# Reordered start rows, a seventh product one step later and copies 32 steps later in a Fourier and token-mixer kernel

## The chip, the cores and the metric

The kernel runs on one core of a Trainium2 chip. The metric is the device time of one execution in microseconds (us). The core has a matrix engine (TensorE, PE in the profile), a vector engine (VectorE, DVE), an activation engine (ScalarE, ACT), GpSimd (POOL) and SyncE (SP), which here only issues DMA transfers. TensorE's weight loads are shown apart as PEld. Each engine works through its own instructions in the order in which the program gives them, and semaphores hold an instruction back until its inputs are there. All transfers share 16 DMA engines.

## The reference

```
xn = layernorm(x)                                    # x: 2048 x 640, over the 640 columns
a = xn @ dft_hid_re.T ;  b = xn @ dft_hid_im.T
fourier = dft_seq_re @ a - dft_seq_im @ b            # 2048 x 640
h = layernorm(xn)
u = gelu(h.T @ w1 + b1)                              # 640 x 1728
mixer = (u @ w2 + b2).T                              # 2048 x 640
out = x + fourier + mixer
```

All arrays are float32.

## The kernel before

Every matrix product is made in three passes (high part times high part, high times low, low times high). ScalarE rounds a 128 x 512 operand to its high part (`high`, line 148), VectorE subtracts to get the low part (`low`, line 151), and TensorE multiplies. Products are grouped by a scheme with seven block products in place of eight; the operands of some are sums or differences of raw blocks, made in place by VectorE (`sub`, line 154). So each raw slice is loaded into `pieces`, perhaps replaced by a difference, then cut into high and low parts.

The work is a list of steps; one step multiplies one cut slice (nine matmuls for products 1, 2, 3 and 5 of a column stage, six for 4, 6 and 7). `turn_of(i)` writes out the work around step i in program order: DMA loads put down for that step, reads of finished PSUM banks, sums, the high part of step i + 2, extras (among them the differences), jobs from a queue, the low part of step i + 2, and last the matmuls of step i. What is late is thus decided by hand-written tables: `JOBS_AT` says in which step of a stage how many queued jobs run, and the numbers in `columns` say when slices are loaded, differences are made and banks are read.

The stages are: a first column block (60 matmuls of 512 columns), written out word by word in the string `START`; eight column stages of the Fourier half (`columns`, g = 0 to 7, 28 steps each, the fourth only 21, beginning at step 5); then hidden-dimension, up and down products. In `columns`, the loads of a stage's slices B11, B21, B12 and B22 are put down from six steps before the stage to four steps into it, into buffers that the stage before frees. The results of a column stage go to DRAM through GpSimd (`store_y`), many of them as accumulating transfers.

In `START`, x k loads row block k of x, b i the i-th first piece and W a slice of the first stage; M and A take a row block's mean and variance on VectorE, R its root on ScalarE, V the factors on GpSimd (four small steps), N normalises the row block, H writes its high part and L its low part; T and B cut piece i into high and low; P multiplies; E and G read finished banks through ScalarE, Y reads them through VectorE; J is a first job of the later sums.

Later row blocks 8 to 15 are loaded in pairs by `later_load` at steps 28, 31, 33 and 35, and their statistics are jobs. The out rows are first filled with x by 16 DRAM-to-DRAM copies of 320 KB on SyncE's queue (line 1174); everything else is accumulated into them later. All SyncE transfers stand in one queue, and the queue holds at an instruction that waits: for a buffer to be freed, or for the transfer eight places before it to land, since eight completion semaphores are used in turn.

Of the kernel before, what the change touches and what calls it, by code (L numbers as in the profile page):

```python
# [11 lines left out]
AF = mybir.ActivationFunctionType  # L12
# [15 lines left out]
H2 = D // 2  # L28
# [15 lines left out]


START = """
    x0 b0 b1 x4 b2 b3 x1 x2 W1-1-0 x3 W1-1-1 x5 W1-1-2 W1-1-3 x6 W2-1-0 x7 W2-1-1 W2-1-2 W2-1-3 W1-2-0 W1-2-1
    M0 A0 R0 T0 D0 O0 V0 H0 B0 M4 A4 T1 B1 N0 R4 T2 L0 O4 V4 H4 B2 P0-0-1 P1-0-1 P0-2 P1-2
    M1 A1 N4 R1 V1 T3 M2 A2 L4 R2 V2 M3 A3 B3 H1 R3 V3 P2 N1 M5 A5 R5 V5 L1 E0-2 T4 B4 P3
    E2-5 T5 N3 M6 A6 R6 V6 H2 B5 T6 N2 M7 A7 P4 B6 R7 V7 J0-0 H3 T7 L2 Y0-1 L3  # L50
    W1-2-2 W1-2-3 W2-2-0 B7 P5 P6 T8 H5 N5 B8 P7 P8 J0-1 T9 N6 Y1-2 B9 G2-3 L5 W2-2-1 T10 H6 J0-2 N7 B10 W2-2-2
    W2-2-3 T11 L6 G3-5 B11 H7 L7 X9 P9
"""

# [2 lines left out]
def jobs_at(ahead, behind=(), light=()):  # L57
    return tuple({i: at.count(i) for i in at} for at in (ahead, behind, light))


JOBS_AT = (
    jobs_at((5, 6, 7, 8, 9, 10, 11, 12, 13, 14, 15, 16, 16, 16, 17, 17, 18, 19, 19, 20, 20, 25, 27)),
    jobs_at((0, 1, 3, 4, 6, 7, 10, 12, 13, 14, 15, 18, 19, 20, 21, 22, 23, 26, 27), (2, 3, 5)),
    jobs_at((0, 1, 2, 3, 4, 5, 41), (0, 1, 2, 3)),
    jobs_at((0, 1, 2, 3, 4, 13, 18, 19, 22, 27), (), (10, 14, 21)),
# [10 lines left out]
def fnet_plus_mixer(  # L76
# [30 lines left out]
    nc = tc.nc  # L107
# [17 lines left out]
    out_rows = [out[t * P : (t + 1) * P, :] for t in range(NS)]  # L125
    x_rows = [x[t * P : (t + 1) * P, :] for t in range(NS)]
# [26 lines left out]
    def sub(to, a, b):  # L153
        nc.vector.tensor_sub(to, a, b)  # L154
# [20 lines left out]
    loads, sums, reads, extras, timed, behind_lo = (defaultdict(list) for _ in range(6))  # L175
# [297 lines left out]
    def c_tile():  # L473

        i = c_turn[0] = (c_turn[0] + 1) % 6
        return c_place[i // 3][:, i % 3, :]

    def store_y(add, m, c, j, t):
        if not add:
            nc.gpsimd.dma_start(y_part[m][c][:, j, :], t)  # L480
        else:
            nc.gpsimd.dma_start(y_part[m][c][:, j, :], t, accum_op=ALU.add)  # L482

    def first_columns():
# [3 lines left out]
        banks = {}  # L488
# [17 lines left out]
                    stop=n == 2 and k == end, skip_group_check=True,  # L506
                )

        def read(m, js, by_vector=False):
            for j in js:  # L510
                c = c_tile()
                if by_vector:
                    nc.vector.tensor_copy(c, banks[m, j])
                else:
                    nc.scalar.activation(c, banks[m, j], AF.Copy)
                store_y(False, m, 0, j, c)

        kept = []
# [52 lines left out]
        def whole_row(k):  # L571
# [15 lines left out]
            "Y": lambda a, b: read(1, range(a, b), True),  # L587
# [4 lines left out]
    def columns(g, h, c, qs=range(4)):  # L592
# [5 lines left out]
        banks, cs = {}, {}  # L598
# [3 lines left out]
        def at(normal, shorter):  # L602
            return s0 + (shorter if short else normal)
# [14 lines left out]
        def b(name, q, n=1):  # L618
            i, m = int(name[1]) - 1, int(name[2]) - 1
            t = raw[m][:, i]  # L620
            return t[:, q, :] if n == 1 else t[:, q : q + n, :]


        order = [(i, q) for i in (1, 2, 5, 6) for q in qs]
        order += [(3, q) for q in qs[:2]] + [(7, q) for q in qs] + [(3, q) for q in qs[2:]]
        order += [(4, q) for q in qs]
        operand = {1: "B11", 2: "B21", 5: "B11", 6: "B11", 3: "B22", 7: "B12", 4: "B21"}
        for names, normal, shorter in (
            (("B11", "B12", "B11"), (5, 7), (3, 4)), (("B12", "B22", "B12"), (6, 8) if g else (13, 15), (5, 6)),
            (("B11", "B22", "B11"), (9, 11), (6, 7)),  # L630
            (("B21", "B21", "B11"), (16, 17) if g else (21, 23), (11, 12)),
        ):
# [45 lines left out]
        def fresh(name, when, key, e, then=None, add=add_all, urgent=False):  # L678
            def run():
                cs[name, e] = c_tile()  # L680
                nc.scalar.activation(cs[name, e], banks[key, e], AF.Copy)
                if then:
                    store_y(add, *then, cs[name, e])

            (reads if urgent or last else extras)[when].append(run)

        def more(name, when, key, e, then):
            if name in by_dram:
                return fresh(name, when, key, e, then, True, name == "C22")

            def run():
                c = cs[name, 0 if name == "F" else e]
                nc.vector.tensor_add(c, banks[key, e], c)  # L693
                store_y(add_all, *then, c)
            reads[when].append(run)

        def first(name, when, key, e, then):
            fresh(name, when, key, e, then if name in by_dram else None)

        first("F", at(4, 3), "f", 0, (0, c, 4))  # L700
        for e in range(2):
            first("C11", at(4, 3) + e, "z", e, (0, c, e))
            more("C11", at(12, 9) + 2 * e, "w", e, (0, c, e))
            first("C22", at(12, 9), "y", e, (1, c, 2 + e))
            first("C12", at(16, 12), "z", e, (1, c, e))
            more("C12", at(24, 18) + e, "y", e, (1, c, e))
            more("C22", at(22, 17) + e, "z", e, (1, c, 2 + e))
            fresh("C21", at(28, 21), "z", e, (0, c, 2 + e))
        more("F", at(10, 7), "f", 1, (0, c, 4))
        fresh("F", at(26, 19), "f", 0, (1, c, 4))  # L710
# [442 lines left out]
    timed[FIRST_STEP].append(lambda: jobs.extend(first_sums[q][j] for q, j in (  # L1153
        (1, 0), (1, 1), (2, 0), (2, 1), (3, 0), (3, 1), (1, 2), (2, 2), (3, 2), (0, 3), (1, 3),
        (0, 4), (0, 5), (1, 4), (1, 5), (2, 3), (2, 4), (2, 5), (3, 3), (3, 4), (3, 5),
    )))
# [142 lines left out]
```

## Time and profile before

| quantity | value |
|---|---|
| median of 3 runs | 869.92 us (869.62 to 869.95) |
| the profiled execution | 868.91 us |
| its span | 867.0 us |
| TensorE busy | 860.4 us, 99% |
| VectorE, ScalarE, GpSimd busy | 693.1, 531.7, 182.2 us |
| TensorE clock granted | 1.00 |
| DMA moved | 158.91 MB, mean 183 GB/s |

In rows of engines' work the first number is the start in us from the span's start, the second the duration in us, and the bracket at the end the idle time before it with what ended it. In rows of waits the columns are the total, the number of waits and the longest. In rows of stretches there follow, after the stretch and its length, busy time and instruction count of PE, PEld, DVE, ACT and POOL, the granted clock, the busy share of the DMA engines (which can exceed 1) and GB/s. In rows of DMA issues the columns are the count, the size of each and the median us from issue to landing. SPq stands for SyncE's queue.

### The profile page before, as it was taken

To read this page: it belongs to the slowest core of one execution; us is meant where nothing else is said; L and a number is where in the kernel's file an instruction comes from. 1 tells how busy PE (TensorE), PEld (TensorE's weight loads), DVE (VectorE), ACT (ScalarE), POOL (GpSimd) and SP (SyncE) were. 2 spreads that over 40 slices of the span, in tenths; PEclk is the share of its full clock that TensorE was granted. 3 is DMA by queue.
4 is the path that set the end of the run, shared out by engine and by line. 5 is a ranking of instruction groups with operands and counts; after the bars stand their busy time and mean duration, and the time that the engine had idled before them with its cause. 6 is when DMAs were issued, how large, how long until landed. Compare 5 with 4: busy or idle time off the path is not lost.

```text
span 867.0 us, 13948 instructions
## 1 busy us (share of the span) xinstructions
PE 860.4 (99%) x4888; PEld 787.3 (91%) x4888; DVE 693.1 (80%) x1171; ACT 531.7 (61%) x993; POOL 182.2 (21%) x255
## 2 busy tenths in 40 slices
PE   8999999999999999999999999999999999999998
PEld 6887888888888888889999999999999999999998
DVE  6997868774757888787877788888678978887887
ACT  6865676765444555647565556676667866555654
POOL 5432222232120211222110101111312221101211
PEclk9999999999999999999999999999999999999999
DMA  9489694979684755869586766665688779766776
GB/s 336 186 213 359 152 310 137 255 144 266 173 245 79 186 116 115 201 114 207 123 177 156 160 140 203 188 170 161 144 186 182 162 216 246 182 141 129 157 168 146
DMA packets 92742, 158.91 MB, mean 183 GB/s; under 512 B 9280, under 2 KB 37696, under 8 KB 92416
## 3 DMA queue, kind: packets, MB, share of 16 engines
q0 software_dynamic: 27456, 61.98, 39.2%
q1 hardware_dynamic: 65072, 95.97, 33.9%
q8 instruction: 38, 0.62, 0.3%
q14 instruction: 32, 0.26, 0.1%
q10 hardware_dynamic: 144, 0.08, 0.0%
HBM read 99.96 MB, written 63.28 MB: 188 GB/s over the span
## 4 chain that ended last, share of the span: by engine, by line
PE 95%; DMA 3%; DVE 1%; POOL 1%; ACT 0%; issue 0%; SPq 0%; DVEq 0%; ACTq 0%
PE psum L160 32%; PE psum L159 32%; PE psum L162 31%; DMA pair<-in_x 1%; DMA pieces<-in_dft_seq 1%; DMA x<-in_x 1%; PE psum L504 0%; DVE st L220 0%; DVE piece L151 0%; POOL beside L245 0%; DVE pieces L154 0%; POOL norm L240 0%; ACT n L275 0%; ACT near L229 0%; SPq L493 0%
## 5 line engine op out<-in xcount | busy, mean ns | idle before, releaser
L148 ACT ACTIVATE piece<-pieces 128x512 fp32r<-128x512 f32 (+3 forms) x487 | 304.8, 626 | 229.5 <-PE psum L162 144.3
L151 DVE TENSOR_TENSOR piece<-pieces,piece 128x512 fp32r<-128x512 f32 (+4 forms) x511 | 336.9, 660 | 135.4 <-ACT piece L148 133.0
L160 PE MATMUL psum<-piece,n 128*128 128x512 f32 x558 | 218.0, 391 | 0.4 <-DVE piece L151 0.4
L162 PE MATMUL psum<-piece,n 128*128 128x512 f32 x558 | 217.5, 390 | 0.0
L159 PE MATMUL psum<-piece,n 128*128 128x512 f32 x558 | 217.4, 390 | 0.0
L160 PEld LDWEIGHTS psum<-piece,n 128*128 128x128 f32 x558 | 104.8, 188 | 24.3 <-DVE piece L151 2.7
L482 POOL DMA_DIRECT2D y<-c x82 | 70.6, 915 | 256.6 <-DVE c L693 130.4
L159 PEld LDWEIGHTS psum<-piece,n 128*128 128x128 f32 x558 | 104.8, 188 | 21.7
L162 PEld LDWEIGHTS psum<-piece,n 128*128 128x128 f32 x558 | 104.8, 188 | 21.4
L160 PE MATMUL psum<-sup,piece 128*128 128x320 f32 x392 | 121.0, 310 | 0.0
L160 PE MATMUL psum<-sdown,piece 128*128 128x320 f32 x392 | 121.0, 310 | 0.0
L159 PE MATMUL psum<-sup,piece 128*128 128x320 f32 x392 | 120.9, 309 | 0.0
L159 PE MATMUL psum<-sdown,piece 128*128 128x320 f32 x392 | 120.9, 309 | 0.0
L154 DVE TENSOR_TENSOR pieces<-pieces 128x512 f32<-128x512 f32 (+3 forms) x146 | 115.7, 797 | 5.8 <-DMA pieces<-in_dft_seq 2.8
L162 PE MATMUL psum<-sup,piece 128*128 128x320 f32 x368 | 113.9, 310 | 0.0
L162 PE MATMUL psum<-sdown,piece 128*128 128x320 f32 x368 | 113.9, 310 | 0.0
L159 PE MATMUL psum<-shid,piece 128*128 128x320 f32 x280 | 86.8, 310 | 0.0
L162 PE MATMUL psum<-shid,piece 128*128 128x320 f32 x280 | 86.7, 310 | 0.0
L160 PE MATMUL psum<-shid,piece 128*128 128x320 f32 x280 | 86.6, 309 | 0.0
L159 PEld LDWEIGHTS psum<-sup,piece 128*128 128x128 f32 x392 | 73.6, 188 | 0.0
L160 PEld LDWEIGHTS psum<-sup,piece 128*128 128x128 f32 x392 | 73.6, 188 | 0.0
L160 PEld LDWEIGHTS psum<-sdown,piece 128*128 128x128 f32 x392 | 73.6, 188 | 0.0
(124 smaller groups left out, 1079.1 us busy)
## 6 DMA issues: line engine op xcount, KB each, us to landing
pieces<-in_dft_seq SPq DMA_DIRECT2D x128, 256.0 KB, 6.0
y<-c POOLq DMA_DIRECT2D x122, 256.0 KB, 6.3
pieces<-in_w SPq DMA_DIRECT2D x88, 256.0 KB, 3.7
out<-pair POOLq DMA_DIRECT2D x38, 320.0 KB, 5.5
pieces<-y SPq DMA_DIRECT2D x32, 320.0 KB, 4.5
pieces<-in_w SPq DMA_DIRECT2D x32, 192.0 KB, 2.6
out<-in_x SPq DMA_DIRECT2D x16, 320.0 KB, 7.6
up<-pair POOLq DMA_DIRECT2D x8, 640.0 KB, 3.6
```

Of the source, the lines that this page charges most:

```text
L148: nc.scalar.activation(hi, src, AF.Copy)
L151: nc.vector.tensor_sub(lo, src, hi.bitcast(F32))
L154: nc.vector.tensor_sub(to, a, b)
L159: nc.tensor.matmul(psum, wh, mh, start=first, stop=False, skip_group_check=True)
L160: nc.tensor.matmul(psum, wh, ml, start=False, stop=last and wl is None, skip_group_check=True)
L162: nc.tensor.matmul(psum, wl, mh, start=False, stop=last, skip_group_check=True)
L482: nc.gpsimd.dma_start(y_part[m][c][:, j, :], t, accum_op=ALU.add)
```

## The change

Five things move. In `START`, the load of row block 4 goes ahead of the second piece; row 1's root and factors go ahead of row 4's normalisation; the statistics of rows and low parts around them are reordered, with the first two bank reads (E0-2) ahead of row 5's root. The two words Y, by which VectorE reads one bank each, are gone, and ScalarE reads these banks too. In the first column stage (g = 0), product 3 takes three slices ahead of product 7 in place of two, so product 7 begins a step later, one half of the differences for it is made two steps later and a bank read one step later; the jobs of the stage's steps 16 to 18 are spread differently and one job of the third sums comes sooner. The 16 copies are put down 32 steps later (steps 67 to 124 in place of 35 to 92).

```
-    x0 b0 b1 x4 b2 b3 x1 x2 W1-1-0 x3 ...
+    x0 b0 x4 b1 b2 b3 x1 x2 W1-1-0 x3 ...
-    M1 A1 N4 R1 V1 T3 M2 A2 L4 R2 V2 M3 A3 B3 H1 R3 V3 P2 N1 M5 A5 R5 V5 L1 E0-2 T4 B4 P3
+    M1 A1 R1 V1 N4 M2 A2 L4 T3 R2 V2 H1 M3 A3 B3 N1 R3 V3 P2 L1 M5 A5 E0-2 R5 V5 T4 B4 P3
...
-    jobs_at((5, 6, 7, 8, 9, 10, 11, 12, 13, 14, 15, 16, 16, 16, 17, 17, 18, 19, 19, 20, 20, 25, 27)),
+    jobs_at((5, 6, 7, 8, 9, 10, 11, 12, 13, 14, 15, 16, 17, 17, 18, 18, 18, 19, 19, 20, 20, 25, 27)),
...
-        order += [(3, q) for q in qs[:2]] + [(7, q) for q in qs] + [(3, q) for q in qs[2:]]
+        n = 2 if g else 3
+        order += [(3, q) for q in qs[:n]] + [(7, q) for q in qs] + [(3, q) for q in qs[n:]]
...
-            (("B11", "B12", "B11"), (5, 7), (3, 4)), (("B12", "B22", "B12"), (6, 8) if g else (13, 15), (5, 6)),
+            (("B11", "B12", "B11"), (5, 7), (3, 4)), (("B12", "B22", "B12"), (6, 8) if g else (13, 17), (5, 6)),
...
-            more("C22", at(22, 17) + e, "z", e, (1, c, 2 + e))
+            more("C22", at(22 if g else 23, 17) + e, "z", e, (1, c, 2 + e))
...
-        loads[s_rows + 30 + 8 * (t // 2) + t % 2].append(lambda t=t: nc.sync.dma_start(out_rows[t], x_rows[t]))
+        loads[s_rows + 62 + 8 * (t // 2) + t % 2].append(lambda t=t: nc.sync.dma_start(out_rows[t], x_rows[t]))
```

ScalarE's instructions around rows 1 and 4 at the start, before and after: `near` is a row's root, x0 a row normalised in place, n01 the high part of row 1, a piece the high part of a piece, c a bank read.

```order
 L275 ACTIVATE n00_116<-x0_75,near_74 128x128
+L229 ACTIVATE near_74<-mv_71,eps_69 128x1
 L275 ACTIVATE x0_75<-x0_75,norm_72 128x640
-L229 ACTIVATE near_74<-mv_71,eps_69 128x1
-L148 ACTIVATE piece_223<-pieces0_120 128x512
+L148 ACTIVATE piece_229<-pieces0_120 128x512
 L229 ACTIVATE near_74<-mv_71,eps_69 128x1
 L275 ACTIVATE n01_117<-x0_75,norm_72 128x256
 L275 ACTIVATE n01_117<-x0_75,norm_72 128x128
-L229 ACTIVATE near_74<-mv_71,eps_69 128x1
 L275 ACTIVATE x0_75<-x0_75,norm_72 128x640
 L229 ACTIVATE near_74<-mv_71,eps_69 128x1
```

Row 1's root moved ahead of row 4's normalisation; the last root in these rows, row 3's after the change, was row 5's before, which now follows two bank reads.

VectorE's instructions where the first stage turns from product 3 to product 7: piece_589 and piece_602 are the first two slices of product 3 in both; piece_614 (before) and piece_631 (after) are the first slice of product 7, piece_613 (after) the third slice of product 3; n is a row sum's low part.

```order
-L154 TENSOR_TENSOR pieces0_120<-pieces0_120 128x1024
 L151 TENSOR_TENSOR n01_117<-x0_75,n01_117 128x256
 L154 TENSOR_TENSOR x0_75<-x0_75 128x256
 L151 TENSOR_TENSOR piece_602<-pieces0_120,piece_602 128x512
-L151 TENSOR_TENSOR n00_116<-x0_75,n00_116 128x256
-L151 TENSOR_TENSOR piece_614<-pieces0_120,piece_614 128x512
-L151 TENSOR_TENSOR n01_117<-x0_75,n01_117 128x256
 L151 TENSOR_TENSOR n02_118<-x0_75,n02_118 128x256
 L154 TENSOR_TENSOR x0_75<-x0_75 128x256
```

The subtraction of two slices left the place ahead of product 3's second slice, and product 7's first slice left the place behind it. After the change these stand in the following rows.

```order
+L151 TENSOR_TENSOR piece_613<-pieces0_120,piece_613 128x512
+L154 TENSOR_TENSOR pieces0_120<-pieces0_120 128x1024
+L151 TENSOR_TENSOR n00_116<-x0_75,n00_116 128x256
+L151 TENSOR_TENSOR piece_631<-pieces0_120,piece_631 128x512
+L151 TENSOR_TENSOR n01_117<-x0_75,n01_117 128x256
```

A third slice of product 3 and the subtraction now stand ahead of product 7's first slice.

SyncE's queue from the end of the fourth column stage to the loads of hidden-dimension matrices, before (pieces are stage slices, the last pieces0 are B12 and B22 of the fifth stage):

```order
L1174 DMA out<-in_x 16x5120
L607 DMA pieces1_121<-in_dft_seq 128x512 x9
L607 DMA pieces0_120<-in_dft_seq 128x512 x8
L782 DMA hids_1978<-in_dft_hid 128x640 x6
L607 DMA pieces0_120<-in_dft_seq 128x512 x4
```

The same part of the queue after:

```order
L1171 DMA out<-in_x 16x5120 x2
L603 DMA pieces1_121<-in_dft_seq 128x512 x6
L1171 DMA out<-in_x 16x5120
L603 DMA pieces1_121<-in_dft_seq 128x512 x2
L603 DMA pieces0_120<-in_dft_seq 128x512
L1171 DMA out<-in_x 16x5120
L603 DMA pieces0_120<-in_dft_seq 128x512 x7
L779 DMA hids_1974<-in_dft_hid 128x640 x2
L1171 DMA out<-in_x 16x5120 x2
```

Six copies came into this part; two of them stand among the slices of the fifth stage, ahead of seven of its eight B12 and B22 slices.

More of the change, by code (lines that the diff above doesn't have):

```diff
@@ L46 @@
 START = """
-    x0 b0 b1 x4 b2 b3 x1 x2 W1-1-0 x3 W1-1-1 x5 W1-1-2 W1-1-3 x6 W2-1-0 x7 W2-1-1 W2-1-2 W2-1-3 W1-2-0 W1-2-1
+    x0 b0 x4 b1 b2 b3 x1 x2 W1-1-0 x3 W1-1-1 x5 W1-1-2 W1-1-3 x6 W2-1-0 x7 W2-1-1 W2-1-2 W2-1-3 W1-2-0 W1-2-1
     M0 A0 R0 T0 D0 O0 V0 H0 B0 M4 A4 T1 B1 N0 R4 T2 L0 O4 V4 H4 B2 P0-0-1 P1-0-1 P0-2 P1-2
-    M1 A1 N4 R1 V1 T3 M2 A2 L4 R2 V2 M3 A3 B3 H1 R3 V3 P2 N1 M5 A5 R5 V5 L1 E0-2 T4 B4 P3
-    E2-5 T5 N3 M6 A6 R6 V6 H2 B5 T6 N2 M7 A7 P4 B6 R7 V7 J0-0 H3 T7 L2 Y0-1 L3
-    W1-2-2 W1-2-3 W2-2-0 B7 P5 P6 T8 H5 N5 B8 P7 P8 J0-1 T9 N6 Y1-2 B9 G2-3 L5 W2-2-1 T10 H6 J0-2 N7 B10 W2-2-2
+    M1 A1 R1 V1 N4 M2 A2 L4 T3 R2 V2 H1 M3 A3 B3 N1 R3 V3 P2 L1 M5 A5 E0-2 R5 V5 T4 B4 P3
+    N3 E2-5 T5 M6 A6 R6 V6 H2 B5 T6 N2 M7 A7 P4 B6 R7 V7 J0-0 H3 T7 L2 G0-1 L3
+    W1-2-2 W1-2-3 W2-2-0 B7 P5 P6 T8 H5 N5 B8 P7 P8 J0-1 T9 N6 B9 G1-3 L5 W2-2-1 T10 H6 J0-2 N7 B10 W2-2-2
     W2-2-3 T11 L6 G3-5 B11 H7 L7 X9 P9
@@ L507, in products, with read @@
                 )
-        def read(m, js, by_vector=False):
+        def read(m, js):
             for j in js:
                 c = c_tile()
[L512 to L515, printed above, removed]
+                nc.scalar.activation(c, banks[m, j], AF.Copy)
                 store_y(False, m, 0, j, c)
@@ L586, in first_columns @@
             "X": lambda i: [f() for f in extras.pop(i)],
-            "Y": lambda a, b: read(1, range(a, b), True),
             "G": lambda a, b: read(1, range(a, b)), "J": lambda q, j: first_sums[q][j](),
@@ L1153, in fnet_plus_mixer @@
     timed[FIRST_STEP].append(lambda: jobs.extend(first_sums[q][j] for q, j in (
-        (1, 0), (1, 1), (2, 0), (2, 1), (3, 0), (3, 1), (1, 2), (2, 2), (3, 2), (0, 3), (1, 3),
-        (0, 4), (0, 5), (1, 4), (1, 5), (2, 3), (2, 4), (2, 5), (3, 3), (3, 4), (3, 5),
+        (1, 0), (1, 1), (2, 0), (2, 1), (3, 0), (3, 1), (1, 2), (2, 2), (3, 2), (0, 3), (1, 3), (2, 3),
+        (0, 4), (0, 5), (1, 4), (1, 5), (2, 4), (2, 5), (3, 3), (3, 4), (3, 5),
     )))
```

## The prediction

> **What bounds the kernel now.** I read the page's busy times first, then the waits of TensorE, then the matmul counts of the stretches in which TensorE loses time, and last the timelines of the engines and queues behind those losses.
>
> ```profile
> PE 860.4 (99%) x4888; PEld 787.3 (91%) x4888; DVE 693.1 (80%) x1171; ACT 531.7 (61%) x993; POOL 182.2 (21%) x255
> ...
> PE psum L504 <- ACT piece L148: 1.3, 1, 1.3
> PE psum L160 <- DVE piece L151: 0.4, 1, 0.4
> PE psum L504 <- ACT c L515: 0.2, 1, 0.2
> ...
> 17.23:20.90 3.67, 3.48 (x14) 2.37 (x13) 2.80 (x8) 3.67 (x10) 3.07 (x9) 1.00 1.06 388
> 49.63:55.51 5.88, 5.88 (x25) 4.35 (x24) 5.88 (x14) 4.36 (x10) 1.98 (x3) 1.00 0.92 218
> 82.73:85.49 2.76, 2.33 (x10) 1.61 (x9) 2.76 (x5) 0.93 (x2) 0.12 (x1) 1.00 1.01 416
> 200.00:300.00 100.00, 100.00 (x443) 82.75 (x442) 67.79 (x93) 49.10 (x85) 19.64 (x23) 1.00 0.74 187
> ```
>
> TensorE is the bound nearly everywhere. A matmul's shown end is modelled, so I count starts: the last row has 443 in 100 us, 0.226 us each, at clock 1.00, and that is the undisturbed pace. The three rows above it are the only stretches worth naming that are slower. Each count includes one matmul that began before the window, so 13, 24 and 9 should take 2.9, 5.4 and 2.0 us. They took 3.67, 5.88 and 2.76. The losses are 0.7 us (TensorE waits for ScalarE to read two banks), 0.5 us (VectorE late with lower parts) and 0.7 us (VectorE late once more): 1.9 us in all, 0.2% of the run. Almost everything else that the change can do is to cost time.
>
> **The bank reads (first row's root sooner).** Before, ScalarE normalises row 4 and only then takes row 1's root; the factors of row 1 go through four GpSimd steps, and ScalarE waits for them.
>
> ```profile
> 11.14 0.21 DVE L223 BATCH_NORM_AGGREGATE mv<-st 128x2 f32<-128x12 f32 x1
> ...
> 11.57 0.92 ACT L275 ACTIVATE x<-x,norm 128x640 f32<-128x640 f32 x1 [0.77 <-POOL norm L240]
> 12.39 0.28 ACT L229 ACTIVATE near<-mv,eps 128x1 f32<-128x1 f32 x1
> 15.10 0.99 ACT L275 ACTIVATE n<-x,norm 128x256 fp32r<-128x256 f32 x2 [1.72 <-POOL norm L240]
> 16.19 0.91 ACT L275 ACTIVATE x<-x,norm 128x640 f32<-128x640 f32 x1
> 17.18 1.53 ACT L515 ACTIVATE c<-psum 128x512 f32<-128x512 f32 x3
> ...
> 12.78 0.70 POOL beside L245
> 14.29 0.79 POOL norm L240
> 17.28 0.49 ACT c L515
> 17.81 3.26 PE psum L504 x12
> ```
>
> Row 1's moments are there at 11.35, so its root can start at 11.4 instead of 12.39, 1.0 us sooner. The GpSimd steps took 12.78 to 15.08, 2.3 us; begun at 11.7 they end near 14.0. Meanwhile ScalarE has row 4 (0.92), so nothing is lost on it. Then 15.10 to 17.18 is repeated from 14.0, without the 0.18 of the root that now stands behind the first two bank reads (17.00 to 17.18): the reads start at 15.9 and the two end at 16.9, before TensorE comes at 17.23. Bounds: a faster chain only adds slack; with all four steps as long as the one at 14.29 (0.79 each, 3.2 us) the reads start near 16.8 and 0.6 of the wait stays. I take the whole 0.7 us as gone. Row 5's factors come about 2 us later behind two store issues; their users stand after 24 us.
>
> Row 4 ahead of the second piece in the queue is worth next to nothing. Its moments start when VectorE gets free.
>
> ```profile
> 2.60 4.58 DMA x<-in_x
> 7.21 0.90 DVE st L220 x2
> ...
> 6.43 0.72 DVE L151 TENSOR_TENSOR piece<-pieces,piece 128x512 fp32r<-128x512 f32 x1 [1.04 <-ACT piece L148]
> 6.69 0.62 ACT L148 ACTIVATE piece<-pieces 128x512 fp32r<-128x512 f32 x1
> ```
>
> VectorE is busy to 7.15 and the row lands at 7.18, so 0.06 us is the most to be had. The second piece takes the row's place, lands near 7.2, and ScalarE's step on it slips from 6.69 by 0.5 us; row 4's root then slips 0.2. TensorE has ten products of the first piece (2.3 us from 6.45), which cover it. Net nothing; without that cover, 0.5 us lost.
>
> **VectorE's share of 20 to 56 us.**
>
> ```profile
> 23.32 0.68 DVE L513 COPY c<-psum 128x512 f32<-128x512 f32 x1
> ...
> 51.03 1.22 DVE L154 TENSOR_TENSOR pieces<-pieces 128x1024 f32<-128x1024 f32 x1
> ```
>
> VectorE runs late in this stretch without a pause (5.88 of 5.88 above). Two bank copies of 0.68 us leave it and go to ScalarE, which has room (4.36 of 5.88). The two-slice subtraction (1.22 us) moves two steps back, three jobs of one step are spread, and a step of nine matmuls (2.0 us) replaces one of six (1.4) where VectorE was late. I take all 0.5 us as gone; the bounds are 0 and 0.5. TensorE would then stand 1.2 us further at 55.5.
>
> **The seventh product, and why the early gain is given back.** The loads of the next stage's first slices wait until VectorE has cut the seventh product's slices, and everything in SyncE's queue waits behind them, the late rows of x included.
>
> ```profile
> 53.77 0.69 DVE L151 TENSOR_TENSOR piece<-pieces,piece 128x512 fp32r<-128x512 f32 x1
> ...
> 54.52 0.33 SPq L607 DMA_DIRECT2D pieces<-in_dft_seq  x1
> 70.52 0.99 SPq L411 DMA_DIRECT2D pair<-in_x  x2
> ...
> 65.00:70.00 5.00, 5.00 (x23) 4.14 (x23) 3.60 (x8) 3.98 (x7) 2.26 (x3) 1.00 1.07 274
> 75.00:80.00 5.00, 5.00 (x23) 4.13 (x23) 3.24 (x8) 2.18 (x5) 0.00 (x0) 1.00 1.04 403
> ...
> 80.82 0.89 DVE L220 BATCH_NORM_STATS2 st<-pair 128x6 f32<-128x320 f32 x2 [2.06 <-DMA pair<-in_x]
> 82.86 0.65 DVE L151 TENSOR_TENSOR piece<-pieces,piece 128x512 fp32r<-128x512 f32 x1
> ```
>
> The queue opens at 54.5, when the cut that began at 53.77 ends, and from 65 to 80 the DMA engines have no free time (shares 1.07 and 1.04). The last pair of rows lands at 80.8, VectorE has stood 2.06 us for it, and the cut for TensorE's step comes behind the statistics, at 82.86. This is the third loss. Now the seventh product moves a step later (+2.0 us), TensorE is 1.2 us ahead, and VectorE has about 1 us less to do before it: its first cut ends at about the same 54.5 (I reckon 53.8 to 55.0). The queue therefore opens at about the old time, the DMA engines are as full as before, and the pair lands at about 80.8. The copies that leave this part stood behind the pair in the queue and do not bring it sooner. So TensorE arrives 1.2 us earlier at a wait that ends when it did: the 0.7 us loss grows to 1.9, and the net of everything up to 85 us is nil. Bounds: 0.7 us gained (queue opens at 53.8) to 0.5 us lost (at 55.0).
>
> **The copies, 32 steps later.** Eight of the sixteen places coincide with old ones. New are the places from step 99 on, and two of these, steps 107 and 108, fall among the loads of the fifth column stage, ahead of its B12 and B22 slices.
>
> ```profile
> 194.30 16.30 SPq L607 DMA_DIRECT2D pieces<-in_dft_seq  x15
> ...
> 199.00:221.00 22.00, 22.00 (x98) 18.23 (x98) 9.08 (x13) 12.74 (x23) 5.99 (x7) 1.00 1.09 294
> ...
> pieces<-in_dft_seq SPq DMA_DIRECT2D x11, 256.0 KB, 12.9
> ...
> 220.68 1.23 DVE L154 TENSOR_TENSOR pieces<-pieces 128x1024 f32<-128x1024 f32 x1 [2.83 <-DMA pieces<-in_dft_seq]
> 221.82 0.69 DVE L151 TENSOR_TENSOR piece<-pieces,piece 128x512 fp32r<-128x512 f32 x1
> ...
> 222.64 0.42 PE L160 MATMUL psum<-piece,n 128*128 128x512 f32 x1
> ...
> 80.00:85.00 5.00, 4.57 (x20) 3.48 (x19) 4.11 (x9) 2.13 (x5) 1.61 (x3) 1.00 1.08 438
> ...
> out<-in_x SPq DMA_DIRECT2D x16, 320.0 KB, 7.6
> ```
>
> From 199 to 221 us the DMA engines are full (1.09), eleven loads need 12.9 us each to land, and VectorE already waits 2.83 us for B22. Its lower part is ready at 222.51, TensorE's second matmul wants it at 222.64: the spare is 0.13 us. A copy is 320 KB, 327,680 bytes (the page's row is the last of the fence). At the 438 GB/s that moved while copies ran (80 to 85 us) it takes 0.75 us, at the 294 GB/s of this window 1.11 us. The slower figure holds accumulating stores, which a copy is not, so I take 0.75: two copies push B22 back 1.5 us, and TensorE stands 1.5 - 0.13 = 1.4 us. Bounds: nothing, if the loads land in time after all, and 2.2 - 0.13 = 2.1 us. The two copies of steps 99 and 100 leave before the stage's loads, into a slacker stretch, and the four from 115 on precede loads that are wanted only some 30 steps later; both at nothing, with 0.5 us if that cover is gone. What the copies' removal frees before 130 us carries no wait of TensorE.
>
> The Trainium skill (DMA: Bandwidth & Descriptors, Specifications) speaks against the small price: it gives a core about 358 GB/s of HBM, and a copy both reads and writes HBM. By it each copy would be 655,360 bytes, 1.8 us, an estimate from that page, and the wait 3.5 us. The 438 GB/s above, with copies in it, lies over that limit even counted once, so the trace does not agree.
>
> **The sum.** On the profiled execution: -0.7 - 0.5 + 1.2 + 1.4 = +1.4 us on a span of 867.0 and a time of 868.91. That execution was 1.0 us below the median of 869.92, so I add the sum to the median: 871.3 us, 0.16% more. About 0.2%, 1.7 us, is what a measurement of this kernel can tell from no change.
>
> **The rivals.**
>
> 1. The copies are hidden: the loads among them have slack that I do not see, or TensorE's new place relative to the stores leaves room. For it: 16 copies run before without one wait of TensorE on them. Against: the spare of 0.13 us. The early part stays nil: 869.9. Chance 0.14.
> 2. The early gain is kept: the pair of rows lands 1.2 us sooner. For it: VectorE has less to do. Against: full DMA from 65 us. With the new wait: 869.92 - 1.2 + 1.4 = 870.1. Chance 0.12.
> 3. Both, and the third loss goes too: 869.92 - 1.9 = 868.0, faster. Chance 0.06. No more than this can be won.
> 4. Slower, early: the seventh product's step (nine matmuls, 2.0 us) goes whole into the opening of SyncE's queue, because VectorE cuts that product only when TensorE has freed a buffer. The pair lands 2.0 us later and the wait at 83 us grows by as much: 871.3 + 2.0 = 873.3. It decides once the first cut ends after about 55.0 instead of 54.46. Chance 0.10.
> 5. Slower, late: a copy weighs on the memory twice. At the 388 GB/s of the load-only stretch at 17 us, 655,360 bytes are 1.7 us, two are 3.4, the wait 3.3: 869.92 + 3.3 = 873.2. Chance 0.06. This is the page's limit at work.
> 6. The change does not do what it says: the reads of the two banks start no sooner. That costs nothing, for the pair's wait swallows the difference; it lies inside the forecast.
>
> **The numbers.** The forecast has 0.52, with a range of its own from 870.4 (0.7 gained early, 0.2 of the new wait missing) to 872.2 (0.5 lost early, and about half of the 0.7 between cheap and dear copies). The line of slower by over 0.2% is 871.66; about three in ten of the forecast's 0.52 lie beyond it, 0.16. With rivals 4 and 5 that is 0.32. Faster by over 0.2% (under 868.18) is rival 3 alone, 0.06. The rest is 0.62. The range from 869.2 to 872.9 leaves out rival 3 and most of 4 and 5.
>
> **What would show it.** Right: TensorE's wait for bank reads at 17.8 gone; matmul starts at 0.226 us from 49 to 55; the statistics of the pair still starting near 80.8, with a TensorE gap of about 1.9 us there; a new gap of about 1.4 us near 222, behind the subtraction that waits for B22. Wrong: a pair that lands before 80, a gap at 222 under 0.5 us, or a queue that opens after 55.5.

## The result, and the profile after

The changed kernel takes 871.93 us (median of 7 runs, 871.18 to 874.13). The kernel before took 869.62 us in the runs beside it (867.95 to 869.95). The medians lie 2.3 us apart, the means (872.27 and 869.20) 3.1; the ratio of the times is 1.0035, 95% interval 1.0022 to 1.0049: slower. The profiled execution took 871.18 us with a span of 869.3 us, against 868.91 and 867.0 before.

The waits of TensorE, over the whole span of the changed kernel (us in total, times, longest):

```profile
PE 860.8 (99%) x4888; PEld 787.0 (91%) x4888; DVE 692.4 (80%) x1169; ACT 532.9 (61%) x995; POOL 182.5 (21%) x255
...
PE psum L160 <- DVE piece L151: 3.2, 3, 2.4
```

The wait for the banks (L515 before) is gone. The wait for VectorE's lower parts has grown from 0.4 to 3.2 us, in three places. Now the timelines of TensorE, VectorE, ScalarE and SyncE at those places (start, duration, engine, line, what; in brackets the idle time ahead and its releaser):

```profile
15.79 1.06 ACT L512 ACTIVATE c<-psum 128x512 f32<-128x512 f32 x2
...
55.04 0.69 DVE L151 TENSOR_TENSOR piece<-pieces,piece 128x512 fp32r<-128x512 f32 x1
55.79 0.33 SPq L603 DMA_DIRECT2D pieces<-in_dft_seq  x1
82.47 0.89 DVE L220 BATCH_NORM_STATS2 st<-pair 128x6 f32<-128x320 f32 x2 [2.47 <-DMA pair<-in_x]
84.50 0.65 DVE L151 TENSOR_TENSOR piece<-pieces,piece 128x512 fp32r<-128x512 f32 x1
...
82.44 0.39 PE L159 MATMUL psum<-piece,n 128*128 128x512 f32 x1
85.20 0.50 PE L160 MATMUL psum<-piece,n 128*128 128x512 f32 x1 [2.37 <-DVE piece L151]
...
223.21 1.23 DVE L154 TENSOR_TENSOR pieces<-pieces 128x1024 f32<-128x1024 f32 x1 [3.70 <-DMA pieces<-in_dft_seq]
224.07 0.39 PE L159 MATMUL psum<-piece,n 128*128 128x512 f32 x1
225.09 0.50 PE L160 MATMUL psum<-piece,n 128*128 128x512 f32 x1 [0.63 <-DVE piece L151]
```

The bank reads start at 15.79 instead of 17.18. SyncE's queue opens at 55.79 instead of 54.52, right after the cut of 55.04. The pair of late rows is there at 82.47 instead of 80.82, and the two matmul starts beside it stand 2.76 us apart instead of 0.82: with 0.23 us for the matmul itself and 0.11 for the slow one behind the gap, 2.6 us are lost where 0.7 were. Near 224 us the starts stand 1.02 us apart: 0.9 us lost with the 0.11, where nothing was. So 2.6 - 0.7 + 0.9 = 2.8 us are new. TensorE began 0.4 us sooner in this execution (first product at 6.04, before at 6.45), which leaves 2.4 us; the span grew by 2.3.

Where did the early gain go? Counts of matmuls in six stretches, before and then after:

```profile
7.00:17.00 10.00, 10.00 (x45) 1.00 1.04 393
17.00:20.00 3.00, 2.81 (x11) 1.00 1.05 387
20.00:28.00 8.00, 8.00 (x36) 1.00 0.84 322
28.00:36.00 8.00, 8.00 (x37) 1.00 0.61 226
36.00:44.00 8.00, 8.00 (x37) 1.00 0.10 36
44.00:56.00 12.00, 12.00 (x53) 1.00 0.75 149
```

```profile
7.00:17.00 10.00, 10.00 (x46) 1.00 1.04 393
17.00:20.00 3.00, 3.00 (x15) 1.00 1.05 386
20.00:28.00 8.00, 7.78 (x34) 1.00 0.85 329
28.00:36.00 8.00, 8.00 (x34) 1.00 0.61 227
36.00:44.00 8.00, 8.00 (x36) 1.00 0.09 36
44.00:56.00 12.00, 12.00 (x54) 1.00 0.75 152
```

Four matmuls are won from 17 to 20 us, and five lost again by 36 us. Both columns add up to 219: of its lead the changed kernel keeps no more than the 0.4 us by which this execution began sooner. One loss did go: the stretch from 49.63 to 55.51 us, with 25 matmuls in the prediction's first rows, now has 27, which is the full pace.

```profile
49.63:55.51 5.88, 5.88 (x27) 4.66 (x27) 5.88 (x13) 4.20 (x10) 1.98 (x3) 1.00 0.93 231
```

In the stretch of the new loss VectorE's cuts come late, and they wait for ScalarE:

```profile
19.74 0.69 DVE L151 TENSOR_TENSOR piece<-pieces,piece 128x512 fp32r<-128x512 f32 x1 [0.83 <-ACT piece L148]
...
27.77 0.69 DVE L151 TENSOR_TENSOR piece<-pieces,piece 128x512 fp32r<-128x512 f32 x1 [0.83 <-ACT piece L148]
```

A third, of 0.31 us, stands between them. Before, there was one such wait, of 0.75 us. And this is VectorE's time from 6 us to the end of the cut that opens SyncE's queue (the sums of its windows: length, busy), with the group of its cuts in that stretch, before and then after:

```profile
sum 48.52, DVE 45.45; mean DVE 11.36
L151 DVE TENSOR_TENSOR piece<-pieces,piece 128x512 fp32r<-128x512 f32 x23 | 15.6, 682 | 1.9 <-ACT piece L148 1.8
L513 DVE COPY c<-psum 128x512 f32<-128x512 f32 x2 | 1.4, 684 | 0.0
```

```profile
sum 49.73, DVE 45.83; mean DVE 11.46
L151 DVE TENSOR_TENSOR piece<-pieces,piece 128x512 fp32r<-128x512 f32 x24 | 16.5, 688 | 2.8 <-ACT piece L148 2.7
```

The two bank copies (1.4 us) have left VectorE's line, but a 24th cut and what goes with it have come, so it is busy 45.83 us instead of 45.45, not less; and it stands idle 3.9 us instead of 3.1, most of the difference ahead of cuts that wait for ScalarE (2.7 instead of 1.8). Together that is 1.2 of the 1.3 us by which the queue opens later.

### The profile page after: what moved, and what is told of

Read it like the earlier page. It is cut to its first block, busy times and chain, and to the rows that moved or that the text cites. A ratio compares the mean times of both kernels' runs of the same rounds, so it can differ in the third digit from the quotient of the medians.

```text
span 869.3 us, 13954 instructions
## 1 busy us (share of the span) xinstructions
PE 860.8 (99%) x4888; PEld 787.0 (91%) x4888; DVE 692.4 (80%) x1169; ACT 532.9 (61%) x995; POOL 182.5 (21%) x255
## 4 chain that ended last, share of the span: by engine, by line
PE 91%; DMA 5%; DVE 1%; SPq 1%; ACT 1%; issue 0%; POOL 0%; DVEq 0%; ACTq 0%
PE psum L160 31%; PE psum L159 31%; PE psum L162 30%; DMA pieces<-in_dft_seq 4%; DMA pair<-in_x 1%; DVE piece L151 0%; DVE st L220 0%; SPq L603 0%; ACT x L275 0%; DVE n L151 0%; ACT piece L148 0%; ACT c L512 0%; ACT n L275 0%; SPq L411 0%; SPq L538 0%
```

## The experiments

Two theories after the result. **A**: the step put ahead of the seventh product delays SyncE's queue, the queue delays the pair, and the pair alone sets when TensorE goes on near 85 us; the two copies of steps 107 and 108 add the gap near 224 us. **B**: the delay comes of the new opening, which loads ScalarE with two bank reads, or of the copies beside the pair.

**The copies alone**, in the kernel before.

```
- loads[s_rows + 30 + 8 * (t // 2) + t % 2]...
+ loads[s_rows + 62 + 8 * (t // 2) + t % 2]...
```

> The kernel before with one edit of the change: the eight copies start 32 steps later. Theory (the two copies at steps 107 and 108 hold up the rows of B22 behind them): a TensorE gap of 0.7 to 1.4 us appears near 222 us, the wait near 82.7 us stays at 0.7 us, no other wait changes, and the span grows by 0.8 to 1.4 us. Rival (the copies leaving the stretch from 75 to 90 us also ease the pair of late rows): the wait at 82.7 us goes under 0.3 us and the pair is there before 80 us, so that the span grows by 0.2 to 0.7 us only.

Measured: 870.06 us, ratio 1.0012 (1.0003 to 1.0020), 1.1 us more. VectorE's and TensorE's timelines:

```profile
81.22 0.89 DVE L220 BATCH_NORM_STATS2 st<-pair 128x6 f32<-128x320 f32 x2 [2.15 <-DMA pair<-in_x]
...
224.89 0.50 PE L160 MATMUL psum<-piece,n 128*128 128x512 f32 x1 [1.38 <-DVE piece L151]
```

The pair is no sooner (81.22), and the gap near 223 us is there: 1.4 us of waiting in this row, 1.6 us lost in all, a little over the forecast. The span of the profiled execution, 869.1 us, is 2.1 us longer and so past its forecast; the median is within it. Taking the copies out of the stretch from 75 to 90 us does not help the pair.

**The changed kernel with the copies put back.**

```
- loads[s_rows + 62 + 8 * (t // 2) + t % 2]...
+ loads[s_rows + 30 + 8 * (t // 2) + t % 2]...
```

> The changed kernel with the copies put back where they were before, all else as changed. Theory (the later copies cost the gap near 224 us and nothing else): that gap is gone, the 2.65 us gap near 82 us stays between 2.3 and 3.0 us, and the span is 0.7 to 1.1 us shorter than the changed kernel's 869.3 us. Rival (the copies beside the pair made the pair later, so that moving them away paid for part of the lateness): the gap near 82 us grows by 0.5 us or more and the span stays within 0.3 us of 869.3 us.

Measured: 871.53 us, ratio 1.0032 (1.0020 to 1.0044), a span of 869.3 us. The gap near 224 us is down to 0.16 us, but near 82 us two gaps together lose 2.9 us instead of 2.6: the queue opened at 56.03 and the pair came at 82.96. The forecast of the span failed: of the 0.7 us that went at 224, 0.5 had been lost before 89 us, about half of it near 82 and half ahead of that, and 0.2 went behind TensorE's last matmul. Since the copies stand behind the pair in the queue, as the forecast for the change had it, they are not what made it later; the queue had opened 0.24 us later, and the pair took 26.93 us from there instead of 26.68.

**The seventh product's edits alone**, in the kernel before.

```
- order += [(3, q) for q in qs[:2]] + [(7, q) for q in qs] + [(3, q) for q in qs[2:]]
+ n = 2 if g else 3
+ order += [(3, q) for q in qs[:n]] + [(7, q) for q in qs] + [(3, q) for q in qs[n:]]
...  (with the subtraction at 17, C22's last pieces at 23, the job steps and the order of the first sums)
```

> The kernel before with the edits of the seventh product alone (its rows behind three pieces of the third product, its first cut, its sum and the last pieces of C22 a step or more later); the opening and the copies as before. Theory (the step later delays SyncE's queue whatever the opening does): the first cut ends 1.0 to 2.0 us later than before's 54.46 us, the pair of late rows lands by as much later, the TensorE gap near 82 us is 1.7 to 2.8 us against 0.7 us, and the span is 0.7 to 1.7 us longer. Rival (the delay came from the new opening, with ScalarE's two further bank reads, and the step later costs nothing): the first cut ends within 0.4 us of 54.46 us and the gap near 82 us stays under 1.1 us.

Measured: 872.43 us, ratio 1.0040 (1.0029 to 1.0052). Its timelines and one window (busy times, granted clock, DMA share):

```profile
55.37 0.33 SPq L607 DMA_DIRECT2D pieces<-in_dft_seq  x1
82.42 0.89 DVE L220 BATCH_NORM_STATS2 st<-pair 128x6 f32<-128x320 f32 x2 [2.05 <-DMA pair<-in_x]
85.16 0.50 PE L160 MATMUL psum<-piece,n 128*128 128x512 f32 x1 [2.39 <-DVE piece L151]
...
86.00:89.40 3.40, 3.40 (x10) 2.69 (x9) 3.30 (x9) 1.81 (x3) 0.00 (x0) 0.52 1.08 442
```

The queue opens late and the pair lands late with the old opening too, so theory B's first half falls. The queue opens 0.85 us later than before, a little less than forecast, though this execution's first product was 0.5 us sooner; the pair lands 1.6 us later. And VectorE's sum from 6 us to that cut, the same as for the kernel before and the changed one above, shows the work that the step puts ahead of it, 1.1 us more than before:

```profile
sum 49.31, DVE 46.59; mean DVE 11.65
```

The time is more than forecast, for a reason on neither list: behind the gap the granted clock is 0.52 for 3.4 us, ten matmul counts where fifteen fit.

**The opening alone** (row 4's load ahead of the second piece included), in the kernel before.

```
- M1 A1 N4 R1 V1 T3 M2 ... M5 A5 R5 V5 L1 E0-2 T4 B4 P3 ... Y0-1 ... Y1-2 B9 G2-3
+ M1 A1 R1 V1 N4 M2 ... L1 M5 A5 E0-2 R5 V5 T4 B4 P3 ... G0-1 ... B9 G1-3
```

> The kernel before with the new opening list alone (the order of the first goes, and all four banks' second reads on ScalarE). Theory (what the opening gains at 17.8 us is lost again between 20 and 36 us behind ScalarE): the wait at 17.8 us is gone, 0.7 to 1.1 us of new TensorE gaps stand between 20 and 36 us, TensorE is within 0.3 us of before's time by 50 us, the gap near 82 us is 0.4 to 0.9 us, and the span is within 0.5 us of before's 867.0 us. Rival (the opening is a gain that the seventh product's edits spoil): under 0.3 us is lost between 20 and 36 us, the first cut ends 0.5 to 0.8 us sooner, and the span is 0.6 to 1.2 us shorter.

Measured: 868.59 us, ratio 0.9995 (0.9987 to 1.0004), a span of 867.0 us, the same as before. Its count from 28 to 36 us, and the rows of the pair and of TensorE behind it:

```profile
28.00:36.00 8.00, 8.00 (x34) 1.00 0.60 223
...
80.84 0.89 DVE L220 BATCH_NORM_STATS2 st<-pair 128x6 f32<-128x320 f32 x2 [1.61 <-DMA pair<-in_x]
83.58 0.50 PE L160 MATMUL psum<-piece,n 128*128 128x512 f32 x1 [1.09 <-DVE piece L151]
```

34 matmuls instead of 37: the opening by itself loses between 28 and 36 us most of what it won before. The queue opened 0.6 us sooner, at 53.88, yet the pair came at 80.84 as before; TensorE was 0.6 us further on there and stood as much longer, 1.4 us lost in place of 0.7, past the forecast of 0.9. Of these 0.6 us the opening made little: TensorE's first product was 0.5 us sooner in this execution.

**The subtraction put back to step 15**, in the changed kernel.

```
- (("B12", "B22", "B12"), (6, 8) if g else (13, 17), (5, 6)),
+ (("B12", "B22", "B12"), (6, 8) if g else (13, 15), (5, 6)),
```

> The changed kernel with one number put back: the 1.2 us subtraction on B22 stands at step 15 again instead of 17, right ahead of the seventh product's first cut; the seventh product keeps its later step. Theory (SyncE's queue opens later because that subtraction now stands ahead of the cut in VectorE's line): the cut ends about 1.1 us sooner, SyncE's queue opens at 54.4 to 54.9 us instead of 55.7, the pair lands 26.3 to 27.0 us behind that, at 80.8 to 81.8 us, and the TensorE gap near 82 us goes from 2.65 us to 1.0 to 1.9 us. Rival (the later step itself sets the cut's time, since the cut waits for its own place in TensorE's order): the queue still opens at 55.4 us or later and the gap stays over 2.3 us.

Measured: 872.74 us, ratio 1.0041 (1.0029 to 1.0053). VectorE's and SyncE's timelines:

```profile
50.62 1.21 DVE L154 TENSOR_TENSOR pieces<-pieces 128x1024 f32<-128x1024 f32 x1
...
53.03 0.41 DVE L151 TENSOR_TENSOR n<-x,n 128x256 fp32r<-128x256 f32 x1
...
54.30 0.41 DVE L151 TENSOR_TENSOR n<-x,n 128x256 fp32r<-128x256 f32 x1
54.64 0.68 DVE L151 TENSOR_TENSOR piece<-pieces,piece 128x512 fp32r<-128x512 f32 x1
55.38 0.33 SPq L603 DMA_DIRECT2D pieces<-in_dft_seq  x1
82.68 0.89 DVE L220 BATCH_NORM_STATS2 st<-pair 128x6 f32<-128x320 f32 x2 [1.93 <-DMA pair<-in_x]
```

My theory for this run fell. The subtraction is back three cuts earlier, at 50.62, but it is still ahead of the seventh product's cut, at step 15 as at 17, and VectorE has no pause in between. Measured from TensorE's first product, the queue opens at 47.9 to 48.6 us in the five kernels with the old step in the table below and at 49.1 to 50.3 us in the five with the later one, this among them: 48.18 and 49.54 us in the mean. The step later costs 1.4 us; one such set on VectorE (a row sum's low part, a row sum, a cut) takes 1.27 us from 53.03 until the next begins at 54.30. The four kernels with the late rows early, which follow, are not in these groups: their queue opens at 48.4 to 49.4 us, and in two of them, with the new opening and the old step, at 49.1 and 49.3, so the step is not the only thing that can delay it.

**The late rows early**, in the changed kernel and in the one before: four loads issued ahead of the load that waits for the cut.

```
- loads[(28, 31, 33, 35)[q]].append(lambda q=q: later_load(q))
+ loads[(11, 12, 13, 14)[q]].append(lambda q=q: later_load(q))
```

> The changed kernel with the four loads of late rows (eight transfers, the pair among them) issued at steps 11 to 14 instead of 28 to 35, ahead of the transfer that waits for the first cut. Theory (the pair's landing alone sets when TensorE resumes near 85 us): the gap near 82 us goes below 0.3 us, the gap near 224 us stays at about 0.9 us, and the span falls by 2.2 to 2.8 us, to 866.5 to 867.1 us. Rival (the pieces behind the pair in the queue are late as well, and the next of them takes its place): 0.8 us or more is still lost between 78 and 95 us.

> The kernel before with the same one edit, the four loads of late rows at steps 11 to 14. Theory: the 0.7 us gap at 82.7 us goes and nothing comes in its place, so that the span is 0.6 to 0.8 us shorter than 867.0 us. Rival (as for the changed kernel, the pieces behind take its place, or the transfers between 36 and 45 us disturb other work): within 0.3 us of 867.0 us or longer.

Measured: 868.52 us for the changed kernel, ratio 0.9996 (0.9987 to 1.0005), and 868.38 us for the one before, 0.9990 (0.9982 to 0.9999). From the changed kernel's timelines and one of its windows:

```profile
78.31 0.48 DVE L220 BATCH_NORM_STATS2 st<-pair 128x6 f32<-128x320 f32 x1
...
223.16 0.50 PE L160 MATMUL psum<-piece,n 128*128 128x512 f32 x1 [1.88 <-DVE piece L151]
...
220.00:230.00 10.00, 8.12 (x29) 6.19 (x28) 7.95 (x10) 1.90 (x3) 0.79 (x1) 0.83 0.85 337
```

The pair's statistics start at 78.31 with no wait for a transfer, and nothing is lost between 78 and 95 us in either kernel. That one edit takes back all that the change had cost, and in the kernel before it wins a little more than nothing: the interval of 0.9990 just leaves out 1. The span forecast of the changed kernel failed in the profiled execution (869.1 us): TensorE came to B22's place 3.2 us sooner, lost 2.2 us there, and the clock fell behind that gap. Of its eleven runs two more were over 869.4 us, and eight lay from 867.95 to 869.17.

**Only the two copies of steps 107 and 108 moved**, to 101 and 102, in the changed kernel.

```
- loads[s_rows + 62 + 8 * (t // 2) + t % 2]...
+ loads[s_rows + 62 + 8 * (t // 2) + t % 2 - (6 if t in (10, 11) else 0)]...
```

> The changed kernel with only two of its eight copies, those at steps 107 and 108, moved six steps ahead to 101 and 102. Theory (these two, queued ahead of B22's rows, make the gap near 224 us): that gap goes below 0.2 us, the gap near 82 us stays at 2.3 to 3.0 us, and the span is 0.7 to 1.0 us shorter than 869.3 us. Rival (the gap comes of the copies' whole load on the transfers, wherever they stand): 0.5 us or more of it stays, or stands at another place between 205 and 230 us.

Measured: 871.74 us, ratio 1.0028 (1.0018 to 1.0038). In the trace the gap near 224 us is gone altogether, with the other fourteen copies still where the change put them: these two make it. In the times that can't be told from the changed kernel, and the span, 869.8 us, is no shorter as forecast but longer: the gap near 82 us brought a low clock more often than not. TensorE's timeline:

```profile
81.65 0.39 PE L159 MATMUL psum<-piece,n 128*128 128x512 f32 x1
84.56 0.80 PE L160 MATMUL psum<-piece,n 128*128 128x512 f32 x1 [2.53 <-DVE piece L151]
85.16 0.63 PE L162 MATMUL psum<-piece,n 128*128 128x512 f32 x1
85.58 0.63 PE L159 MATMUL psum<-piece,n 128*128 128x512 f32 x1
```

Starts are 0.42 us apart there instead of 0.23. Of this kernel's twelve runs, four have a mean granted clock of 1.000 and take 869.39 to 871.27 us; eight have 0.998 or less and take 871.43 to 874.35 us. The medians lie 1.6 us apart, about what 3.4 us at half speed lose.

**The changed opening with the late rows early**, in the kernel before; and the same with two bank reads left on VectorE.

```
- M1 A1 N4 R1 V1 T3 M2 ...          (the opening list, as above)
+ M1 A1 R1 V1 N4 M2 ...
- loads[(28, 31, 33, 35)[q]]...
+ loads[(11, 12, 13, 14)[q]]...
second kernel:  Y0-1 instead of G0-1, and Y1-2 G2-3 instead of G1-3
```

> The kernel before with the changed opening list (all second bank reads on ScalarE) and the four loads of late rows at steps 11 to 14. Theory (with the pair's wait gone, what the opening gains is no longer swallowed near 82 us): no gap near 82 us, about 0.5 us lost between 20 and 36 us, no wait at 17.8 us, and a span 0.3 to 0.6 us under that of the kernel before with the late rows alone (865.7 us): 865.1 to 865.5 us, with 0.2 to 0.4% off the time before. Rival (something else behind 60 us is paced by transfers and takes the gain back): 865.7 us or more.

> As the run before it, but with two of the bank reads left on VectorE as they were. Theory (the losses between 20 and 36 us come of ScalarE's two more bank reads, for which VectorE's lower parts then wait): VectorE waits for ScalarE's pieces about 0.8 us between 17 and 54 us instead of 2.0, TensorE loses under 0.25 us between 20 and 36 us, and the span is 0.2 to 0.5 us shorter than that of the run before it. Rival (those losses come of the new order of the rows, not of who reads the banks): 0.4 us or more is still lost between 20 and 36 us.

Measured: 868.22 us, ratio 0.9991 (0.9982 to 1.0000), and 868.23 us, ratio 0.9992 (0.9984 to 1.0001). Neither beats the late rows alone (0.9990). The first one's span, 866.6 us, misses its forecast: 1.3 us are lost between 20 and 36 us. In the second VectorE still waits 1.5 us for ScalarE's pieces between 17 and 54 us (2.0 with the reads on ScalarE, 0.8 before), and 0.8 us are lost between 20 and 36 us. That is the rival's sign: under 0.25 us had been forecast, and 0.2 are lost there before. The changed kernel itself loses 0.8 us there and the opening alone 0.7, both with the reads on ScalarE. So the new order of the rows is enough to give the gain back; that the two bank reads have a share in it is not shown, and which of the moves in that order does it was not tried.

**One copy, and four, ahead of the pair**, in the kernel before.

```
- loads[(28, 31, 33, 35)[q]]...                    both kernels
+ loads[(28, 31, 33, 36)[q]]...
- loads[s_rows + 30 + 8 * (t // 2) + t % 2]...      second kernel
+ loads[s_rows + 30 + (0 if t < 4 else 8 * (t // 2) + t % 2)]...
```

> The kernel before with the load of the pair of late rows one step later, which puts one copy (320 KB) ahead of it in SyncE's queue. Theory (TensorE resumes 2.76 us after the pair's first row lands, whatever comes before): the pair lands 0.7 to 0.9 us later for one copy at the rate of 438 GB/s, the gap near 82.7 us grows from 0.7 us to 1.4 to 1.6 us, and the span by 0.7 to 0.9 us. Rival (a copy weighs on the memory twice): 1.4 to 1.9 us on each of these.

> The kernel before with four copies (1.28 MB) ahead of the pair of late rows in SyncE's queue. Theory: four times the price of one, so the pair lands 2.8 to 3.4 us later and the gap near 82.7 us is 3.5 to 4.1 us; and the granted clock falls to about half for some 3 us behind a gap of that length in every run, which costs another 1.4 to 1.7 us: a span of 871.2 to 872.1 us against 867.0. Rival for the price (a copy weighs twice): a gap of 6 us or more. Rival for the clock (the low clock in some runs came of something else than TensorE's gap): granted clock 1.00 behind the gap, and a span of 869.8 to 870.4 us.

Measured: 870.33 us, ratio 1.0024 (1.0014 to 1.0034), and 874.59 us, ratio 1.0069 (1.0056 to 1.0081). VectorE's timeline with one copy, then VectorE's, TensorE's and one window with four:

```profile
82.72 0.89 DVE L220 BATCH_NORM_STATS2 st<-pair 128x6 f32<-128x320 f32 x2 [3.44 <-DMA pair<-in_x]
```

```profile
85.02 0.89 DVE L220 BATCH_NORM_STATS2 st<-pair 128x6 f32<-128x320 f32 x2 [6.21 <-DMA pair<-in_x]
86.41 0.89 DVE L220 BATCH_NORM_STATS2 st<-pair 128x6 f32<-128x320 f32 x2 [0.26 <-DMA pair<-in_x]
...
88.16 0.79 PE L160 MATMUL psum<-piece,n 128*128 128x512 f32 x1 [5.41 <-DVE piece L151]
...
88.15:91.75 3.60, 3.59 (x9) 2.82 (x10) 3.50 (x8) 0.63 (x1) 0.00 (x0) 0.50 0.15 58
```

Put together with the runs above, two spans of time move little, one of them hardly at all:

| profiled kernel | first product | queue opens | pair's statistics | between | TensorE goes on | between |
|---|---|---|---|---|---|---|
| before | 6.45 | 54.52 | 80.82 | 26.30 | 83.56 | 2.74 |
| changed | 6.04 | 55.79 | 82.47 | 26.68 | 85.20 | 2.73 |
| copies alone | 6.24 | 54.87 | 81.22 | 26.35 | 83.96 | 2.74 |
| changed, copies back | 5.78 | 56.03 | 82.96 | 26.93 | 85.70 | 2.74 |
| seventh product alone | 5.96 | 55.37 | 82.42 | 27.05 | 85.16 | 2.74 |
| opening alone | 5.98 | 53.88 | 80.84 | 26.96 | 83.58 | 2.74 |
| changed, subtraction at 15 | 6.20 | 55.38 | 82.68 | 27.30 | 85.42 | 2.74 |
| changed, two copies moved | 5.88 | 55.01 | 81.83 | 26.82 | 84.56 | 2.73 |
| one copy ahead | 6.83 | 55.05 | 82.72 | 27.67 | 85.46 | 2.74 |
| four copies ahead | 6.05 | 54.15 | 85.02 | 30.87 | 88.16 | 3.14 |

Without a copy ahead, the pair comes 26.3 to 27.3 us behind the queue's opening, 26.8 in the mean. In the two kernels with copies ahead, the pair's later step puts one slice load (256 KB) ahead of it as well, so a copy's price is read between these two: three more copies make the span 3.2 us longer, 1.1 us for each. That is more than the 0.75 of the forecast and less than the 1.7 of the rival that counted it twice. The run with one copy by itself would have spoken for that rival, with its pair 1.9 us later than before; but 0.5 us of this is the queue's later opening in that execution, and the rest is hardly clear of the 1.0 us by which the span varies without a copy. With four the gap is 5.6 us, between the forecast of up to 4.1 and the rival's 6.

The span behind the opening is not quite fixed: it is 26.5 us in the mean of the three kernels with the old step and no copy ahead, and 27.0 in the five with the later one. In the changed kernel the DMA engines are less busy from 55 to 65 us than before (shares 0.80 and 0.84, against 0.97 and 0.92), which fits a queue that is held up again behind its opening; what holds it was not tried. TensorE goes on 2.74 us behind the pair's first row, whatever it did before; with four copies the second row came 1.4 us behind the first and sets the end.

For the clock, the five runs with four copies ahead all have a mean granted clock of 0.996 to 0.998, so the low clock did follow the long gap every time.

## Why the prediction was right or wrong

The direction was right and the size short. The measured 871.93 us lies 0.6 us above the 871.3 forecast and within the range, but with 0.35% it is past the 0.2% line, on the side to which I gave 0.32. That the number came so near is in part luck. The part up to 85 us, put at nothing and bounded by a gain of 0.7 and a loss of 0.5, cost 1.5 us in the profiled execution (the 1.9 at the pair less the 0.4 of a sooner start), and the copies cost 0.9 where I had 1.4, so one miss hides some of the other.

- **The bank reads** (-0.7): right. They start at 15.79 where I had 15.9, and the wait at 17.8 is gone.
- **VectorE's share of 20 to 56 us** (-0.5): right for the place named, where TensorE is at the full pace again (27 matmuls from 49.63 to 55.51 us, 25 before), and wrong for the stretch, for this is where the lead went. I took ScalarE's room from the last part (4.36 of 5.88 us busy at 50 to 55); between 20 and 36 us VectorE's lower parts now wait for ScalarE's pieces, and TensorE loses 0.8 us there where it lost 0.2. The run with two bank reads left on VectorE loses as much, so the order of the rows is enough for it, and that I had not priced here. TensorE was to stand 1.2 us further at 55.5. By the counts up to 56 us it stood where it had stood before, apart from its sooner start.
- **The queue's opening** (+1.2 given back, at 54.5): the failed step. I reckoned VectorE 1 us lighter up to the cut and bounded the opening by 55.0; it has 0.4 us more to do and 0.8 us more to wait, and the queue opened at 55.79, past the 55.5 that I had named as a sign of being wrong. What I left out of VectorE's line is the extra slice of the third product and what goes with it: the seventh product alone brings 1.1 us more work ahead of that cut. Rival 4 had the right mechanism and the right point: past 55.0 the step goes into the pair's landing. Its price was 1.3 us at the queue and 1.65 at the pair, not 2.0. Its reason was off: VectorE was busy up to the cut and not waiting for a buffer, so what delays it is the work put ahead of it.
- **The pair sets the end near 83 us**: right, and firmer than I put it (2.74 us in nine kernels). A lead of TensorE is swallowed there as long as the pair comes no sooner, so the 0.7 and the 0.5 could not have reached the end by themselves. A later queue does reach it, 1.3 us at the queue as 1.65 at the pair; a sooner one need not: the opening alone, with its queue 0.6 us sooner, had the pair at the old time.
- **The copies** (+1.4 near 222): the mechanism was right and the two copies named were the ones. The changed kernel's execution lost 0.9 us; the three other profiled kernels with these copies at steps 107 and 108 lost 1.6 to 2.2. At the price measured above, two copies less the spare of 0.13 are 2.0. So 1.4 lies in the middle, though the price of a copy under it was too low; what makes the gap vary from 0.9 to 2.2 stays open. In the times this part can't be seen within the change: the changed kernel without that gap has ratios of 1.0032 (copies back) and 1.0028 (two copies moved).

By the HBM limit of the Trainium skill (DMA: Bandwidth & Descriptors, Specifications), with a copy's bytes counted twice, a copy takes 1.8 us, the estimate of the prediction; the runs with one and four copies ahead of the pair have 1.1, so these runs do not agree with it.

- **Row 4 ahead of the second piece** (nothing): not tried by itself; the opening as a whole is worth nothing that can be measured (0.9995, 0.9987 to 1.0004).

The sum of the forecast, -0.7 - 0.5 + 1.2 + 1.4, comes out in the trace as 0 (opening and VectorE's share together, by the counts), +1.9 at the pair, +0.9 at B22, and -0.4 of a sooner start: +2.4 on the profiled execution, whose time is 2.3 us longer. The times that the single parts cost alone (1.1 for the copies, 3.4 for the seventh product, -0.4 for the opening) add up to 4.1 and not to the change's 2.3 (3.1 by its ratio). Four of the seventh product's five runs have a mean granted clock of 0.998, and of the changed kernel's seven only one has under 0.999; that is a part of it, and the rest stays open.

## What to carry to other kernels

Before counting a gain, look for the next wait whose end is set by something the gain does not touch; here a load behind a blocked queue ended the wait, and the lead before it was worth nothing. When work is put ahead of an instruction that opens a queue, add up that engine's line to that instruction, its waits included, since busy engines have no slack to absorb a step. And a load that nobody blocks belongs ahead of the one that waits: moving four loads took back all that the change had cost.

## What the runs showed of the hardware

The granted clock of TensorE falls to about half behind gaps that lose 2 to 3 us, in some executions and not in others, for some 3 to 3.6 us; eight matmuls at 0.43 us instead of 0.23 then cost 1.6 us. In the profiles a loss of 2.7 us at one place (two copies moved) was followed by it, one of 2.6 us (changed kernel) was not, and one of 2.2 us (late rows early) was; the gap of 5.6 us with four copies had it in five runs of five. The Trainium skill (TensorE: Matmul & The Clock Gate, Part 1: The HAM clock gate) has the clock halved after an idle window of about 3.4 us, on a free-running grid of such windows. The length of the slow stretch agrees with these 3.4 us. That gaps well under 3.4 us already bring it does not agree: here gaps of 2.2 to 2.7 us were not safe from it.
